# Block 1's inverse transform split twice, one of its sums moved to an accumulating transfer, and a new order of all engines

## The chip, the cores and the metric

The kernel runs on one core of one Trainium2 chip. The core has a matrix engine (TensorE, PE in the profile; its weight loads are PEld), a vector engine (VectorE, DVE), a scalar engine (ScalarE, ACT), a GpSimd engine (POOL) and SyncE (SP), which only issues transfers. Matmuls write to PSUM, and ACT or DVE carry results from there to SBUF ("evacuate"). Sixteen DMA engines move data for all queues. The metric is device time in microseconds for one execution; lower is better.

## The reference, cut to what matters

S = 2048 tokens, D = 640 channels, F = 1728. A long convolution (done with a Fourier transform) is followed by a gated FFN; each has a layer norm in front and a residual around it.

```python
def _A_ref(q, k, v, shift_k, ssm_k, ssm_D):
    k_shift = sum of k delayed by 0..3 tokens * shift_k          # four taps
    kv = k_shift * v
    y = irfft(rfft(pad(kv)) * rfft(pad(ssm_k)))[:S]               # causal long convolution
    y = y + kv * ssm_D
    return q * y
x = A_q
h = x + _A_ref(_layernorm(x), A_k, A_v, A_shift_k, A_ssm_k, A_ssm_D)
g, u = silu(_layernorm(h) @ w_gate), _layernorm(h) @ w_up
h2 = h + (g * u) @ w_down
```

## The kernel before

**Tiling.** The sequence is cut into four blocks of 512 tokens (numbers 0 to 3), and so is the convolution kernel. Each block is transformed by matmuls with a cosine and sine table into 512 complex frequencies, and the output of block i is the inverse transform of the sum over j of X(j) * C(i-j), where C are combined transforms of the convolution kernel's blocks. Within a block, token 4p + j sits on partition p in row j (j = 0 to 3). The frequencies are held in four groups of 128, one frequency per partition, each with a real and an imaginary plane, so a group of one block is 2 x 640 elements per partition, and a whole block 8 x 640 = 5120.

**Splitting.** A transform of 512 tokens can be split by the parity of the rows: the even and odd rows are transformed on their own into half of the frequencies, and sums and differences (a butterfly) give the rest. Split once, the inverse transform of a tile of 128 tokens needs 8 matmuls of 320 columns; split twice, it needs 4, and more additions. `iquads` (line 639) writes the additions of the inverse split twice; the list `R4Y` (line 360) names the blocks that use it: 2 and 3. Blocks 0 and 1 are split once: since the list `MB` (line 350) holds all blocks, `prod` (line 772) adds two DVE operations of 2560 elements by `bfly` (line 558) at the end of the block's products. They are called yb1.0 and yb1.1 for block 1. `inverse` (line 900) then has 8 or 4 matmuls per tile (lines 924 and 919).

**Sums by transfer.** `addto` (line 567) gives a sum dst += src to an accumulating transfer from SBUF to SBUF on POOL's queue instead of an addition on DVE. The list `LO` (line 343) names butterflies of which one sum is done so. For an inverse split twice that is named there, the four groups come out in another place: with the entry, tiles of rows 1 and 3 read groups that the transfer does not write, rows 0 and 2 the groups that it writes (line 905), and iquads reads those for its last difference (5) before the transfer (4) adds to them.

**Tasks and their names.** The work is recorded as a list of tasks, each numbered in the order of its creation, with the memory that it reads and writes; waits are worked out from that (`add`, line 92; `emit`, line 180). The names used here, for block i, kernel block m, row or tile j:

- `k0t`, `k0e`: transposes of the first block of K and their evacuations; `kt`/`kte`: transposes of the convolution kernel's blocks and their evacuations (1280 elements).
- `kf`/`kfe`: the forward transform of kernel block m, eight tasks of 4 matmuls, and their evacuations; `kb`: its butterflies; `kc`: combination to C.
- `tp`/`ke`/`kv`: taps by matmul, their evacuation, the product with v (DVE, line 742); `xf`/`xfe`/`xb`: forward transform of block i, its evacuations and butterflies (block 1 to 3: eight tasks of 2 matmuls; block 0: of 8).
- `pji`: the products X(j) * C(i-j) on DVE (line 777); `p02.e` and others with `e` are accumulations by transfer. `yb`: the inverse's butterfly.
- `iv`: inverse transform of a tile, then `e` evacuation (ACT), `g` gate with the normed x and residual (DVE), `m`, `s` mean and square sum (ACT, lines 840 and 842), `v`, `r` (DVE, and a power on POOL, line 837), `n` normalize (DVE), `ht` transpose to the FFN's layout (SP). For blocks 0 and 1, position 1 is row 2 and position 2 is row 1 (line 876).
- `la`/`lp`: the layer norm in front of the convolution, `lar` its power on POOL.
- `fg`, `fu`: gate and up matmuls (line 1029; 20 matmuls of 256 columns, 15 in the last group, for two halves of the block's tokens, named by the first digit after the point), `sg`, `su`, `sv`: silu and copy (ACT), `mu`: product (DVE, line 1050), `gd` a small copy; `dn`: down projection (line 1115; 28 matmuls of 320 columns), `rs`, `ra`: residual (DVE or ACT, and an accumulating transfer), `out`: store (SP).

**Order.** No engine chooses: the table `PLAN` (line 256) holds for each of the five engines the full list of task numbers in the order in which it issues them, and so also which engine does a task that two could do (for instance an evacuation). PSUM is used as four units of two banks; "units" in the table gives the unit of each PSUM tile, and a task that opens a tile waits until the last tile in that unit is evacuated. "fills" adds matmuls without use in front of a task, to keep PE running. `ub`, the buffer of the up projection, exists once: `su` waits for the `mu` before it. The order of the stages (line 348) is

```python
SEQ = "P01 K W F0 S1 P11 I1 P02 P12 P03 P13 F1 S2 P22 I2 P23 F2 S3 P33 I3 F3"
```

P stands for products, K for kernel block 3, W for the weights, F for the FFN, S for a block's loads, taps, forward transform and norm, I for its inverse. This is the order of creation; PLAN interleaves the stages, so that F0 on PE runs beside S1 and P11 on ACT and DVE.

Of the kernel before, what the change touches and what calls it, by code (L numbers as in the profile page):

```python
# [50 lines left out]
class _Graph:  # L51
# [128 lines left out]
    def emit(self, block):  # L180
# [74 lines left out]

PLAN = {
# [9 lines left out]
    "act":  # L266
# [10 lines left out]
    "dve":  # L277
# [10 lines left out]
    "pool":  # L288
        "19 17 15 16 125 165 174 158 192 183 223 225 224 342 396 362 281 371 285 401 380 289 406 389 343 293 420 415 527 466 "
        "470 561 474 552 478 579 570 684 586 591 529 705 710 698 637 732 723 641 645 750 649 741 "  # L290
        "",
    "sp":
        "0 2 3 8 4 6 10 7 230 9 11 13 14 235 296 226 12 229 297 227 481 231 167 176 228 234 295 233 194 185 482 232 364 282 373 "
        "290 391 294 286 382 480 653 652 471 563 554 467 475 479 581 572 651 734 725 638 752 646 743 642 650 798 807 801 804 "
        "810 "
        "",
    "units":
        "0131203132312001201201213230032110213023012230313133033220021021122013200230230222110332013110130232003210332301202110"
        "01310112312301210312031012210230131023033303012010313012013"
        "",  # L300
    "fills": {
        "wb0": ["zmem", 3],
        "k0t4.0": ["zmem", 1],
    },
}

# [1 line left out]
def bass_sequential_preLN__ssm_conv_h3__swiglu_ffn__prompt_kernel(  # L308
# [31 lines left out]
    DA = ((1,2),(1,3),(2,3),(3,3))  # L340
    KD = (3,)
    DD = (2,)
    LO = (('k',2),('k',3),('x',3))
    RD = (0,1,2)
    KS = (1,)
    TS = ((3,3),)
# [10 lines left out]
    HALF = (0, 1, 2, 3)  # L357
    R4K = ()
    R4X = (1,2,3)
    R4Y = (2,3)  # L360

    Q = N // 2
    kf = np.arange(Q).astype(np.float64) + 0.25
# [15 lines left out]
    with ExitStack() as es:  # L379
# [178 lines left out]
        def bfly(name, e_, o_, lo, hi, n, inplace=True, part=2):  # L558
            ops = [(hi, ALU.subtract), (lo, ALU.add)][:part]
            for k, (d, op) in enumerate(ops if inplace else ops[::-1]):  # L560
                g.add("%s.%d" % (name, k), "dve", lambda e, q, d=d, op=op: e.tensor_tensor(out=d, in0=e_, in1=o_, op=op), ("sb", n),
                      r=[e_, o_], w=[d])
# [4 lines left out]
        def addto(name, dst, src):  # L567
            return g.add(name, "pool", lambda e, n: e.dma_start(dst, src, accum_op=ALU.add, max_dma_last_dim=4096), ("acc", 2 * int(np.prod(dst.shape))),  # L568
                         r=[dst, src], w=[dst], dma=True)
# [38 lines left out]
        def quads(name, src, dst, tmp, scale, rot):  # L608
            low = (name[0], int(name[2])) in LO
            ev = 2 if low else 0  # L610
# [28 lines left out]
        def iquads(i):  # L639
            y = Y[i]  # L640

            def two(f0, c0, step):
                a = y[:, f0, c0]
                return bass.AP(a.tensor, a.offset, [list(a.ap[0]), [step * D, 2], [1, D]])

            tt2 = (("0", OS[:, 0], y[:, 0], y[:, 2], ALU.add, 2), ("1", OS[:, 1], y[:, 0], y[:, 2], ALU.subtract, 2),
                   ("2", y[:, 0], y[:, 1], y[:, 3], ALU.add, 2), ("3", y[:, 2], two(1, 1, 3), two(3, 1, -5), ALU.subtract, 2),
                   ) + ((("5", y[:, 1:4:2], OS[:], y[:, 0:3:2], ALU.subtract, 4),) if ("y", i) in LO else (
                   ("4", y[:, 1:4:2], OS[:], y[:, 0:3:2], ALU.add, 4), ("5", y[:, 0:3:2], OS[:], y[:, 0:3:2], ALU.subtract, 4)))
            for q, d, a, b, op, n in tt2:  # L650
                g.add("yb%d.%s" % (i, q), "dve", lambda e, n_, d=d, a=a, b=b, op=op: e.tensor_tensor(out=d, in0=a, in1=b, op=op), ("sb", n * D),
                      r=[a, b], w=[d])
            if ("y", i) in LO:
                addto("yb%d.4" % i, y[:, 0:3:2], OS[:])

        def kfwd(m, dst):
# [6 lines left out]
            halves("kf%d" % m, KT[m], dst, KO, D ** 0.5 / N, m)  # L663
            if ("k", m) in LO:
                bfly("kb%d" % m, dst[:, 0:2], KO[:], dst[:, 0:2], dst[:, 2:4], 4 * D, part=1)
# [87 lines left out]
        def xfwd(i):  # L753
# [7 lines left out]
            halves("xf%d" % i, kvo, x, OS, 1.0, i)  # L761
            if ("x", i) in LO:
                bfly("xb%d" % i, x[:, 0:2], OS[:], x[:, 0:2], x[:, 2:4], 4 * D, part=1)
# [8 lines left out]
        def prod(j, i):  # L772
# [3 lines left out]
            def op2(nm, d, a, b, op, n):  # L776
                g.add(nm, "dve", lambda e, n_: e.tensor_tensor(out=d, in0=a, in1=b, op=op), ("sb", n * D), r=[a, b], w=[d])  # L777
# [20 lines left out]
            for f2 in range(2):  # L798
# [13 lines left out]
                elif j:  # L812
                    op2(nm + "e", yy, yy, tacc[odd], ALU.add, 4)
                if i == j and i not in FULLY + R4Y and ("y", i) not in MB:
                    bfly("yb%d.%d" % (i, f2), y[:, f2], y[:, f2 + 2], OS[:, f2], y[:, f2 + 2], 2 * D, False)
            if i == j and i in R4Y:
                iquads(i)
            elif i == j and ("y", i) in LO:
                g.add("yb%d.0" % i, "dve", lambda e, n: e.tensor_tensor(out=OS[:], in0=y[:, 0:2], in1=y[:, 2:4], op=ALU.subtract), ("sb", 4 * D),
# [80 lines left out]
        def inverse(i):  # L900
            hold = [None]
            for j in (0, 2, 1, 3) if i in JP else range(4):
                pt = g.tile()

                full = i in FULLY
                src = Y[i][:] if full else Y[i][:, ((0, 2, 1, 3) if ("y", i) in LO else (1, 3, 0, 2))[j]] if i in R4Y else (OS[:], Y[i][:, 2:4])[(j + (("y", i) in LO)) % 2]

                def mm(e, n, pt=pt, j=j, src=src, full=full):
                    if full:
# [5 lines left out]
                        return last  # L915
                    if i in R4Y:
                        for cs in range(2):
# [10 lines left out]
                nm = "iv%d.%d" % (i, pos(i, j))  # L928
                g.add(nm, "pe", mm, ("mm", W, 16 if full else 4 if i in R4Y else 8), r=[itab[:], src] + ([nitab[:]] if full else []), pw=[pt])
                x, s = xh[i % 2][:, j, :], st1[i % 2]  # L930
# [295 lines left out]
```

## Time and profile before

| | us |
|---|---|
| three timed runs | 259.1, 260.73 (median), 261.67 |
| profiled execution, its own time | 259.3 |
| its span, first to last instruction | 257.3 |
| between them | 2.0 |

The profile is of one execution. Its rows give the start and the length in microseconds from the start of the span, the engine, the line of the kernel, and what is written and read, by the names of buffers without their number (Y, C, XH are the transforms, OS and KO scratch, ps is PSUM). In rows of the timeline a bracket gives the idle time of the engine before the row and what ended it. In the chain that ended last, a row's time is counted from the end of the row before, so that rows there are the spacing of instructions, a little less than their length: an operation of 2560 elements on DVE has a length of 1.48 and a spacing of 1.40. PE's matmuls overlap, so a busy PE need not be one that issues at its fastest.

### The profile page before, as it was taken

The numbers are of one execution on the slowest core, as the hardware profiler recorded it, in microseconds if no ns is written. First come the engines' busy times: TensorE is split into PE (matmuls) and PEld (weight loads), VectorE is DVE, ScalarE is ACT, GpSimd is POOL, SyncE is SP. The second block draws the span as 40 slices with busy tenths as digits, with TensorE's granted clock in tenths as the row PEclk, the third lists the DMA queues.
The fourth block names the chain that finished last, engine by engine and source line by source line (L and its number), as shares of the span: only waits on it lengthen the run. The fifth ranks groups of instructions, "written<-read, shape, count | busy, mean of one in ns | idle before, by whom it ended". The sixth has DMA issues, their size and how long they took to land.

```text
span 257.3 us, 5303 instructions
## 1 busy us (share of the span) xinstructions
PE 249.3 (97%) x2253; PEld 195.1 (76%) x2253; DVE 200.0 (78%) x256; ACT 184.5 (72%) x302; POOL 58.5 (23%) x56
## 2 busy tenths in 40 slices
PE   7999997999999999979999999999999999999995
PEld 4878773587888766868888866788886678888763
DVE  3689999999999998999999988999958524211242
ACT  2489999999996894577899789749981854516410
POOL 1001003082312052860030813333230314000000
PEclk9999999999999999999999999999999999999999
DMA  6998946788994058786946035497870152700011
GB/s 220 335 328 210 402 155 133 221 205 190 329 190 87 0 82 124 128 164 153 273 87 124 3 51 117 118 221 133 148 135 3 25 104 33 149 0 3 0 42 60
DMA packets 37620, 35.29 MB, mean 137 GB/s; under 512 B 21203, under 2 KB 32478, under 8 KB 37598
## 3 DMA queue, kind: packets, MB, share of 16 engines
q1 hardware_dynamic: 31792, 23.82, 33.2%
q0 software_dynamic: 5792, 11.14, 25.1%
q8 instruction: 17, 0.28, 0.5%
q14 instruction: 5, 0.04, 0.1%
q10 hardware_dynamic: 14, 0.01, 0.0%
HBM read 16.55 MB, written 2.62 MB: 75 GB/s over the span
## 4 chain that ended last, share of the span: by engine, by line
PE 62%; DVE 20%; ACT 11%; DMA 5%; issue 1%; SPq 0%; DVEq 0%
PE ps L1029 32%; PE ps L1115 16%; DVE tt L777 6%; PE ps L599 3%; DMA Y<-tt 3%; DVE Y L777 3%; PE ps L731 2%; ACT KO L455 2%; PE ps L919 2%; ACT C L455 2%; PE ps L581 2%; DVE C L777 2%; PE ps L992 2%; PE ps L619 2%; DMA k0n<-in_A_k_dram 1%; DVE gu L1050 1%
## 5 line engine op out<-in xcount | busy, mean ns | idle before, releaser
L1115 PE MATMUL ps<-Wd,gu 128*128 128x320 bf16 (+1 forms) x420 | 58.7, 300 | 0.0
L1115 PEld LDWEIGHTS ps<-Wd,gu 128*128 128x128 bf16 (+1 forms) x420 | 38.7, 97 | 18.4 <-issue 3.6
L777 DVE TENSOR_TENSOR tt<-XH,C 128x2560 bf16<-128x2560 bf16 (+1 forms) x31 | 47.8, 1571 | 1.5 <-DMA Y<-tt 0.9
L1050 DVE TENSOR_TENSOR gu<-gu,ub 128x1024 bf16<-128x1024 bf16 (+1 forms) x32 | 19.8, 620 | 26.2 <-ACT gu L1037 13.7
L1037 ACT ACTIVATE gu<-ps 128x1024 bf16<-128x1024 f32 (+1 forms) x32 | 29.4, 923 | 12.1 <-PE ps L1029 12.0
L1029 PE MATMUL ps<-hnT,GB 128*128 128x256 bf16 x280 | 34.0, 273 | 0.9 <-ACT XT L455 0.9
L1042 ACT ACTIVATE ub<-ps 128x1024 bf16<-128x1024 f32 x24 | 24.6, 1024 | 13.3 <-PE ps L1029 11.5
L1029 PE MATMUL ps<-hnT,UB 128*128 128x256 bf16 x280 | 33.8, 273 | 0.0
L1029 PEld LDWEIGHTS ps<-hnT,GB 128*128 128x128 bf16 x280 | 27.3, 98 | 4.3 <-ACT XT L455 1.0
L1029 PEld LDWEIGHTS ps<-hnT,UB 128*128 128x128 bf16 x280 | 27.3, 98 | 3.4 <-ACT KO L455 0.2
L1029 PE MATMUL ps<-hnT,GA 128*128 128x256 bf16 x240 | 28.8, 273 | 0.0
L1029 PE MATMUL ps<-hnT,UA 128*128 128x256 bf16 x240 | 28.5, 273 | 0.1
L837 POOL TENSOR_TENSOR mv<-mv,half 128x1 f32<-128x1 f32 x16 | 21.3, 1335 | 24.7 <-DVE mv L835 24.7
L1029 PEld LDWEIGHTS ps<-hnT,UA 128*128 128x128 bf16 x240 | 23.4, 98 | 3.4 <-ACT C L455 0.5
L1029 PEld LDWEIGHTS ps<-hnT,GA 128*128 128x128 bf16 x240 | 23.4, 98 | 3.2 <-DVE XH L458 0.3
L840 ACT ACTIVATE qo<-xh 128x640 bf16<-128x640 bf16 x28 | 21.0, 749 | 5.7 <-DMA xh<-in_A_q_dram 3.2
L581 PE MATMUL ps<-KT,tab 128*128 128x320 bf16 x128 | 19.6, 300 | 1.6 <-ACT K3r L455 0.7
L934 ACT ACTIVATE qo<-ps,one,st 128x640 bf16<-128x640 f32 x16 | 13.7, 886 | 9.8 <-PE ps L919 9.0
L568 POOL DMA_DIRECT2D xh<-RB x12 | 10.7, 888 | 34.7 <-DVE RB L1132 23.2
L581 PEld LDWEIGHTS ps<-KT,tab 128*128 128x128 bf16 x128 | 11.5, 98 | 8.2 <-ACT K3r L455 1.6
L837 POOL TENSOR_TENSOR st<-st,half 128x4 f32<-128x4 f32 x4 | 7.9, 1986 | 33.6 <-DVE st L832 21.8
L455 ACT ACTIVATE XH<-ps 128x640 bf16<-128x640 f32 x19 | 13.3, 736 | 1.5 <-PE ps L619 0.7
(112 smaller groups left out, 384.8 us busy)
## 6 DMA issues: line engine op xcount, KB each, us to landing
C<-US POOLq DMA_DIRECT2D x6, 640.0 KB, 5.9
kc<-in_A_ssm_k_dram SPq DMA_DIRECT2D x4, 640.0 KB, 10.6
xh<-in_A_q_dram SPq DMA_DIRECT2D x4, 640.0 KB, 5.5
out_dram<-xh SPq DMA_DIRECT2D x15, 160.0 KB, 2.0
kvo<-in_A_v_dram SPq DMA_DIRECT2D x3, 640.0 KB, 4.4
xh<-RB POOLq DMA_DIRECT2D x12, 160.0 KB, 3.0
Wd<-in_B_w_down_dram SPq DMA_DIRECT2D x1, 1280.0 KB, 7.8
C<-K3r POOLq DMA_DIRECT2D x2, 640.0 KB, 7.9
```

The lines of the kernel that those rows point to most:

```text
L455: return e.activation(out=dst[1], in_=src(), func=ACTF.Copy, scale=scale)
L568: return g.add(name, "pool", lambda e, n: e.dma_start(dst, src, accum_op=ALU.add, max_dma_last_dim=4096), ("acc", 2 * int(np.prod(dst.shap ...
L581: last = e.matmul(pt.f(c, W), tab[:, f, cs, j], src[:, j, c * W:(c + 1) * W], start=(j == js[0]), stop=(j == js[1]))
L777: g.add(nm, "dve", lambda e, n_: e.tensor_tensor(out=d, in0=a, in1=b, op=op), ("sb", n * D), r=[a, b], w=[d])
L837: g.add(name + "r", "pool", lambda e, n: e.tensor_tensor(out=dst, in0=tmp, in1=hf, op=ALU.pow), ("pp", 4), r=[tmp, half[:]], w=[dst])
L840: g.add(name + "m", "act", lambda e, n: e.activation(out=junk, in_=x, func=ACTF.Identity, scale=-1.0 / D, accum_out=sm), ("aa", D, 0), r=[ ...
L934: g.add(nm + "e", "act", lambda e, n, pt=pt, q2=q2, s=s, j=j: e.activation(out=q2, in_=pt.f2(W), func=ACTF.Identity, scale=s[:, 3, j:j + 1 ...
L1029: last = e.matmul(pt.f(q // 2, 256, o=256 * (q % 2)), w[:, c, f0:f0 + P], hnT[:, c, cols], start=(c == 0), stop=(c == NC5 - 1))
L1037: g.add("sg%d.%d%d" % (i, h, gp), "act", lambda e, n, pa=pa, gv=gv, nf=nf: e.activation(out=gv, in_=pa.f(0, 256 * nf).rearrange("p (f x) - ...
L1042: g.add("su%d.%d%d" % (i, h, gp), "act", lambda e, n, pb=pb: e.activation(out=ub[:].rearrange("p b x -> p (b x)"), in_=pb.f(0, 1024), func ...
L1050: g.add("mu%d.%d%d" % (i, h, gp), "dve", lambda e, n, gv=gv, ubv=ubv: e.tensor_tensor(out=gv, in0=gv, in1=ubv, op=ALU.mult), ("sb", 256 * ...
L1115: last = e.matmul(pt.f(c, W), gu[k, fb, col(i, j)], Wd[k, fb, c * W:(c + 1) * W], start=st, stop=sp)
```

## The change

Two entries in lists change, the filler in front of `k0t4.0` goes, and PLAN is new for all five engines and for the PSUM units. The code of the functions is the same.

```diff
-    LO = (('k',2),('k',3),('x',3))
+    LO = (('k',2),('k',3),('x',3),('y',1))
...
-    R4Y = (2,3)
+    R4Y = (1,2,3)
...
     "fills": {
         "wb0": ["zmem", 3],
-        "k0t4.0": ["zmem", 1],
     },
```

Block 1's butterfly yb1, which was two DVE operations of 2560 elements, becomes five on DVE and one transfer: yb1.0 to yb1.3 of 1280 elements, yb1.5 of 2560, and the accumulation yb1.4 (2560 elements on 128 partitions, 640 KB). Block 1's four inverse tiles have 4 matmuls each in place of 8. As four tasks more are created, all task numbers from 356 on are 4 higher. One list of PLAN shows what such a change looks like (POOL; 359 is yb1.4, 342 is la1r, and 396 before and 400 after is p02.e):

```diff
     "pool":
-        "19 17 15 16 125 165 174 158 192 183 223 225 224 342 396 362 281 371 285 401 380 289 406 389 343 293 420 415 527 466 "
+        "15 17 16 125 174 165 158 183 192 126 223 225 224 342 359 400 281 375 366 285 405 384 289 393 410 343 293 424 419 531 "
...
```

The orders that matter, written out in names. PE, from the taps of block 1 to the FFN of block 0, before:

```
tp1.2 tp1.0 iv0.0 iv0.1 tp1.4 kf2.101 iv0.2 iv0.3 kf3.001 kf2.100 kf2.111 xf1.30 xf1.31 kf2.010 kf2.001 kf2.011 kf2.110
xf1.11 kf2.000 xf1.10 xf1.01 fu0.00 xf1.20 xf1.00 fg0.00 xf1.21 fg0.01 kt3.1 kf3.100 fu0.01 kf3.101 .. kf3.010 fu0.02
```

and after:

```
tp1.0 kt2.0 iv0.1 tp1.4 tp1.2 iv0.0 kf2.001 iv0.3 kf2.111 xf1.00 kf2.011 xf1.01 xf1.31 xf1.21 iv0.2 xf1.10 kf2.010 xf1.11
kf2.101 kf2.000 kf2.100 kf2.110 xf1.30 kt3.0 kt3.1 xf1.20 fg0.00 fu0.00 fg0.01 kf3.000 fu0.01 kf3.100 .. kf3.110 fu0.02
```

ACT follows PE's order; after, kte3.0 and kf3e.001 stand behind sg0.00, and its last tasks before sg0.00 are xf1e.30, kf2e.110, iv0.2m, iv0.3m, xf1e.20, iv0.2s. PE around block 1's inverse, before and after:

```
fu0.10 fu0.12 fu0.11 iv1.1 iv1.0 fg0.13 iv1.3 dn0.0 iv1.2 dn0.0b dn0.1 dn0.2 dn0.3 fu1.00 fg1.00 tp2.2 tp2.0 tp2.4 fg1.02 xf2.30
fu0.11 dn0.0 fu0.12 iv1.1 fg0.13 dn0.0b iv1.3 iv1.0 dn0.1 iv1.2 dn0.3 dn0.2 tp2.4 fg1.00 fu1.00 fu1.01 tp2.0 tp2.2 fg1.01 xf2.30
```

DVE from the products of block 1 on, before and after:

```
p11.1c la1v mu0.02 p11.1e mu0.03 yb1.0 mu0.10 yb1.1 p02.d p02.a iv1.0g p02.c mu0.11 p02.b mu0.12 iv1.1g p12.0b ..
  .. p03.a iv1.2n p03.c mu1.00 kv2.2 kv2.0 kv2.4 p03.d iv1.3n p13.0b
p11.0e kc2.s yb1.1 p11.1b p11.1a p11.1d p11.1c yb1.0 p11.1e mu0.02 la1v yb1.2 yb1.3 mu0.03 yb1.5 mu0.10 p02.d mu0.11 p02.a p02.c p02.b ..
  .. iv1.2n p03.a mu1.00 p03.c kv2.4 p03.d iv1.3n kv2.0 kv2.2 p13.0a
```

Early on, kte0.0, k0e4 and kf0e.011 go from DVE to ACT, k0e0 and kf0e.001 from ACT to DVE, the memset of the filler's operand from POOL to DVE, and the small lp0 from DVE to POOL. On SP, ht1.1 and ht1.0 stand ahead of out0.0 (before: ht1.0, out0.0, ht1.1), and the end is out3.1, out3.2, out2.0, out2.3, out3.0, out2.2, out3.3a, out3.3c (before, the stores of block 2 stood ahead of those of block 3).

More of the change, by code (lines that the diff above doesn't have):

```diff
@@ L257 @@
     "pe":
[7 rows of a table removed]
[7 rows of a table added]
         "",
     "act":
[9 rows of a table removed]
[9 rows of a table added]
         "",
     "dve":
[9 rows of a table removed]
[9 rows of a table added]
         "",
     "pool":
-        "19 17 15 16 125 165 174 158 192 183 223 225 224 342 396 362 281 371 285 401 380 289 406 389 343 293 420 415 527 466 "
-        "470 561 474 552 478 579 570 684 586 591 529 705 710 698 637 732 723 641 645 750 649 741 "
+        "15 17 16 125 174 165 158 183 192 126 223 225 224 342 359 400 281 375 366 285 405 384 289 393 410 343 293 424 419 531 "
+        "470 474 565 478 556 482 583 688 574 590 595 709 714 702 641 727 736 754 645 745 649 653 "
         "",
     "sp":
-        "0 2 3 8 4 6 10 7 230 9 11 13 14 235 296 226 12 229 297 227 481 231 167 176 228 234 295 233 194 185 482 232 364 282 373 "
-        "290 391 294 286 382 480 653 652 471 563 554 467 475 479 581 572 651 734 725 638 752 646 743 642 650 798 807 801 804 "
-        "810 "
+        "0 2 3 8 4 235 6 10 7 9 11 13 227 296 231 12 226 295 297 14 234 228 230 485 176 167 229 233 185 486 194 232 377 368 282 "
+        "290 286 656 294 395 386 484 657 475 567 558 471 479 483 585 655 576 729 738 747 646 756 805 808 642 654 802 650 811 "
+        "814 "
         "",
     "units":
-        "0131203132312001201201213230032110213023012230313133033220021021122013200230230222110332013110130232003210332301202110"
-        "01310112312301210312031012210230131023033303012010313012013"
+        "0123102130122303101303103122223010213301211001312202202021131313332201310122130021331303333002132202031300211201000323"
+        "31110331322013012013201213012023101322020020212010232210321"
         "",
```

50 rows, old and new, of the table PLAN are left out of this document.

## The prediction

> **What bounds the kernel now.** I read the page's busy lines first, then busy time by stretches, then the chain that ended last, and last the timelines of the engines where the chain changes hands. The page:
>
> ```profile
> span 257.3 us, 5303 instructions
> PE 249.3 (97%) x2253; PEld 195.1 (76%) x2253; DVE 200.0 (78%) x256; ACT 184.5 (72%) x302; POOL 58.5 (23%) x56
> ```
>
> Busy time by stretches (time, then PE, PEld, DVE, ACT, POOL, clock, DMA share, GB/s):
>
> ```profile
> 36.00:57.00 21.00, 18.93 (x152) 12.53 (x150) 20.62 (x23) 21.00 (x40) 6.68 (x4) 1.00 0.66 163
> 57.00:82.00 25.00, 25.00 (x228) 21.14 (x226) 24.97 (x28) 23.59 (x41) 7.70 (x6) 1.00 0.88 212
> 82.00:112.00 30.00, 29.12 (x282) 22.00 (x280) 28.53 (x30) 20.53 (x35) 13.54 (x11) 1.00 0.55 86
> 112.00:160.00 48.00, 47.52 (x446) 37.93 (x444) 46.18 (x61) 41.42 (x71) 11.99 (x10) 1.00 0.56 119
> 200.00:257.30 57.30, 54.61 (x454) 42.88 (x451) 16.20 (x30) 24.44 (x40) 5.97 (x8) 1.00 0.22 47
> ```
>
> PE alone looks like the bound, with 8.0 us idle in 257.3. But from 36 to 112 DVE is idle for 1.88 us only (0.38 + 0.03 + 1.47), and ACT for none from 36 to 57. So up to some 160 us three engines are full at once and only the last 57 us belong to PE alone. The chain shows who is really last:
>
> ```profile
> 43.47 0.59 ACT C L455
> ...
> 54.81 0.71 ACT qo L840 x2
> ...
> 56.12 0.92 ACT gu L1037
> ...
> 58.52 0.73 DVE OS L634
> ...
> 77.67 0.59 DVE gu L1050
> ...
> 80.00 1.40 DVE OS L561
> ...
> 81.92 1.48 DVE Y L561
> ...
> 91.64 8.39 DMA Y<-tt
> 100.05 1.50 DVE tt L777
> ...
> 112.87 1.55 DVE kvo L742 x3
> 114.47 0.72 PE ps L619 x4
> 115.19 2.18 PE ps L1029 x20
> ...
> 149.78 1.24 PE ps L919 x8
> ...
> 198.81 1.09 PE ps L919 x8
> ```
>
> The chain runs through ACT until 57, through DVE until 114.4, and only then through PE. Block 1's butterfly (the two L561 rows) is on the DVE part. PE stands still for 2.07 us in the ACT part (18.93 of 21.00) and again where the chain leaves DVE (PE's timeline, in brackets its idle time):
>
> ```profile
> 63.62 2.36 PE L1029 MATMUL ps<-hnT,UB 128*128 128x256 bf16 x20
> ...
> 111.63 2.36 PE L1029 MATMUL ps<-hnT,GB 128*128 128x256 bf16 x20 [0.88 <-ACT XT L455]
> 114.47 0.72 PE L619 MATMUL ps<-kvo,tab 128*128 128x320 bf16 x4 [0.48 <-DVE kvo L742]
> ```
>
> **The change, part by part.** (1) PE. Block 1's inverse falls from 32 to 16 matmuls of 320 columns. Eight take 1.09 us in the chain, so one is worth 0.136 us and the sixteen 2.18 us. This is the only gain in work. The removed filler matmul is costed at 0:
>
> ```profile
> 1.14 3.47 DMA k0n<-in_A_k_dram
> 3.99 0.61 PE L502 MATMUL ps<-gu 128*128 128x512 bf16 x1
> ```
>
> The first rows of K land at 4.61 and the filler ends at 4.60: it stood inside that wait. If its absence mattered it would be by less than its own 0.61 us, in either direction.
>
> (2) DVE. Two operations of 2560 elements (1.40 in the chain, 2.80) become four of 1280 (0.73 to 0.74, 2.94) and one of 2560 (1.40): +1.54 us inside the stretch where DVE has no reserve. Otherwise both orders hold the same DVE tasks between kb0.0, where that stretch begins, and yb2.4, block 2's butterfly sum. What changes is when it begins:
>
> ```profile
> 20.02 1.49 DVE L561 TENSOR_TENSOR C<-C,KO 128x2560 bf16<-128x2560 bf16 x1 [0.18 <-ACT KO L455]
> ...
> 23.74 2.90 DVE L777 TENSOR_TENSOR tt<-XH,C 128x2560 bf16<-128x2560 bf16 x2 [0.26 <-ACT XH L455]
> ...
> 28.53 2.90 DVE L777 TENSOR_TENSOR tt<-XH,C 128x2560 bf16<-128x2560 bf16 x2 [0.29 <-ACT XH L455]
> 31.34 1.56 DVE L777 TENSOR_TENSOR Y<-tt 128x1280 bf16<-128x1280 bf16 x2
> ...
> 100.05 1.49 DVE L777 TENSOR_TENSOR tt<-XH,C 128x2560 bf16<-128x2560 bf16 x1 [0.90 <-DMA Y<-tt]
> ...
> 114.33 1.48 DVE L777 TENSOR_TENSOR C<-tt 128x2560 bf16<-128x2560 bf16 x1
> 115.73 0.44 DVE L981 TENSOR_SCALAR qo<-xh,mv 128x640 bf16<-128x640 bf16 x1
> ...
> 148.22 1.49 DVE L651 TENSOR_TENSOR Y<-OS,Y 128x2560 bf16<-128x2560 bf16 x1
> ```
>
> At 20.02 kb0.0 waits for four of the eight evacuations kf0e. The last of the four is now the seventh and not the eighth: -0.59, one evacuation. At 23.74 and 28.53 DVE waits for ACT's evacuations of xf0, ahead of which fewer evacuations of transposed K are now put: -0.55 for the two waits. The copy that DVE gives to ACT (kte0.0) and the memset that it takes from POOL lie ahead of this stretch and count 0. I take -1.2 in all, with 0 and -1.9 as ends (nothing; one evacuation more). Of later waits I take as many as before, 1.88. Net at yb2.4: +1.54 - 1.2 = +0.3 us.
>
> (3) The place of block 2's k·v products. Before, the three kv2 end at 114.42 (112.87 + 1.55). After, p03.d (1.40) and iv1.3n (0.36, from 115.73 to the next start at 116.09) stand ahead of the last two: 114.42 + 0.3 + 1.76 = 116.5. The forward transform xf2 needs all three. PE does one FFN group more ahead of it (fg1.01 and fu1.01 in place of fg1.02), which costs 2.18 (20 matmuls, the row at 115.19) and uses up just what (1) saved. Without its stalls near tp2.4 and fg1.02 (0.88 and 0.48 idle; some 1.7 from start to start) PE would be there at 114.47 - 1.7 = 112.8; so it waits in the new order too. With that group already done PE leaves this point, on the old scale of work, at 116.5 - 2.18 = 114.3: 0.15 ahead and not 2.18.
>
> (4) ACT between 33 and 66. The old order mixes the eight xf1 with FFN groups; the new one runs iv0, kf2 and xf1 in one piece and FFN behind it, where each xf1 gives PE 0.27 us (2 x 0.136) and ACT 0.59. Ahead of sg0.00 ACT loses kte3.0 (1.13), su0.00 (0.92), iv0.3s (0.81) and kf3e.001 (0.59), and gains kte0.0 (1.13) and iv0.2s (0.81):
>
> ```profile
> 32.60 1.13 ACT KT L455
> ...
> 39.00 0.81 ACT qo L842 x2
> ...
> 52.71 0.92 ACT ub L1042
> ```
>
> That is -1.5, so sg0.00 starts between 54.6 and, if the 1.5 goes in new waits, 56.1; I take 55.0. Evacuation kf2e.110, which frees the PSUM unit for fg0.00, ends 2.8 us earlier (two L840 at 0.71, one evacuation, one L842), at 52.2. From there to fu0.02 PE has four FFN groups (8.72) and eight kf3 (4.37): 65.2. Before it was there at 63.62 with the same tasks done, so it is 1.6 late. In the sum that costs nothing while DVE is the later one at xf2: 112.8 + 1.6 = 114.4 against 116.5. Were DVE early it would cost the 1.6.
>
> (5) The accumulating transfer yb1.4, 640 KB on POOL's queue, stands behind la1r (a power of 4 elements) and ahead of p02.e:
>
> ```profile
> 77.76 1.40 POOL L837 TENSOR_TENSOR st<-st,half 128x4 f32<-128x4 f32 x1 [1.72 <-DVE st L835]
> ...
> 142.60 4.42 POOL L837 TENSOR_TENSOR st<-st,half 128x4 f32<-128x4 f32 x1 [9.58 <-DVE st L835]
> ```
>
> It waits for yb1.5, which reads what it writes. Before, yb1.1 ended at 83.40. Ahead of yb1.5's end DVE has 1.54 more of butterfly, no mu0.10 (0.59) and the earlier start: 83.4 + 1.54 - 0.59 - 1.2 = 83.1. With the 8.39 us of the nearest transfer (same target) it lands at 91.5. PE wants it at iv1.0, ahead of which it has, counted from iv1.1's old start at 82.73, iv1.1 and iv1.3 in half (1.09), fg0.13 (15 x 0.109 = 1.64) and dn0.0 (28 x 0.136 = 3.81): 89.3, and 90.9 with the 1.6 of (4). So PE waits 0.6, or 2.2 if it isn't late, and either way is there at 115.0 for xf2, where (3) swallows it. Behind it p02.e goes out at about its old 91.64, 10 us later. I take 0, ends 0 and +1.1 (the third rival).
>
> Queue SP: the transposes ht1.1 and ht1.0 now stand ahead of the store out0.0, which helps. At the end four stores of block 2 are put behind out3.2, shortly before the last store, on the same queue. I take +0.2, ends 0 and +0.6 (0.15 each).
>
> **Sum.** At iv2.1 (149.78 before) DVE's sum allows 149.8 + 0.3 = 150.1, PE by itself 149.78 - 0.15 = 149.6. So +0.3 there. From there PE's work is the same, its order too but for swaps inside F2 and F3, and the chain stays on PE from there on with hardly a wait, so the shift goes to the end: +0.3 + 0.2 = +0.5. The profiled execution took 259.3 us; that is 1.4 below the median 260.73 of the three runs (259.1, 260.73, 261.67). With it the middle of the four is 260.0, and on that I put the sum: **260.5 us**. A measurement of this kernel can tell about 1%, 2.6 us, from no change.
>
> **Rivals.** *Gain kept.* If DVE loses the 1.88 us that it idled between 36 and 112 and starts 0.7 earlier still, kv2 ends at 113.9 and PE (114.4) is the bound at xf2: on the old scale 112.2 and not 114.47, -2.2. 260.0 - 2.2 + 0.2 = 258.0. For it: PE has no other work added. Against it: half of DVE's idle time is the 0.90 for the transfer Y<-tt, and between p02.e and its waiter DVE has only one more short task (iv1.0g) than before. Chance 0.25.
>
> *DVE waits for ACT* (slower). In (4) ACT delivers just when DVE asks. From the end of the first products (32.9, less 1.2: 31.7) to xb1.0 DVE has seven operations of 1.40, two of 2.74 and short ones, 19.5 in all, so it is there at 51.2; xf1e.30 stands just ahead of kf2e.110 and ends at 52.2 - 0.6 = 51.6. From there each us that ACT is later goes through kv2 and yb2.4 to the end. If the 1.5 of (4) is lost in waits and the kf3 evacuations are late by PE's 1.6 as well: +3.1, or 260.0 + 3.1 + 0.5 = 263.6. For it: ACT is busy for 21.00 of 21.00 us between 36 and 57. Against it: its sum is smaller than before. Chance 0.27.
>
> *The accumulate is late.* One power of this kind took far longer than the rest:
>
> ```profile
> L837 POOL TENSOR_TENSOR mv<-mv,half x16: 540/862/5208, 41.0 to 217.7; 128x1 f32<-128x1 f32 x16
> ```
>
> Then la1r, which starts at about 80, ends at 85.2, the transfer lands at 93.6, 2.7 after PE wants it (90.9). The wait at xf2 swallows 2.1 of that (114.4 against 116.5), 0.6 stays, and I allow 0.5 for the evacuation and the products that queue behind iv1.0 on ACT and DVE: +1.1, or 261.6. Up to 2.1 us late it costs nothing. For it: DVE runs additions without a break behind la1v, as at 142.60. Against it: so it did at 77.76. Chance 0.10. [...]
>
> **Chances.** Forecast 0.38, its own range 259.3 to 262 (the ends of start, accumulate and stores). Over all: 257.6 to 264.0. Faster by over 1% (under 258.1): 0.18, most of the first rival. Slower by over 1% (over 263.3): 0.23, most of the second. Within: 0.59.
>
> **What would show it.** Block 1's inverse in sixteen matmuls; idle time of PE of some 2 us before xf2, ended by DVE kvo; kv2 ending near 116.5; yb2.4's addition ending within 1 us of 150; fu0.02 later than 63.6. Wrong would be: PE without idle time from 100 to 120; DVE idle for over 3 us between 36 and 112; PE waiting over 2 us for the transfer Y<-OS; or idle time of PE after 163, where I count none.

## The result, and the profile after

The changed kernel takes 267.34 us (median of 6 runs, 266.18 to 267.91) against 260.91 us for the kernel before beside it: a ratio of 1.0246, 95% interval 1.0204 to 1.0287. The forecast was 260.5, so it is slower by 6.4 us where almost no change was expected. The profiled execution took 266.18 us, its span is 264.2. Two profiles below (the transfer ahead of la1r, 264.69 us, and the old start, 263.76) are of slow executions, 4 to 5 us above their medians, and are read only up to 142 us. The page:

```profile
span 264.2 us, 5274 instructions
PE 249.6 (94%) x2236; PEld 193.4 (73%) x2236; DVE 201.5 (76%) x260; ACT 184.5 (70%) x302; POOL 66.6 (25%) x56
```

PE has 17 matmuls fewer, and POOL is busy for 8.1 us more with the same 56 instructions. Busy time by stretches (columns as before):

```profile
36.00:57.00 21.00, 18.22 (x144) 12.00 (x143) 20.41 (x23) 20.97 (x39) 6.47 (x4) 1.00 0.70 160
57.00:82.00 25.00, 25.00 (x222) 21.46 (x220) 24.75 (x27) 22.98 (x39) 7.94 (x7) 1.00 0.87 191
82.00:112.00 30.00, 24.85 (x186) 16.98 (x184) 25.03 (x29) 18.31 (x33) 15.87 (x11) 0.89 0.57 93
112.00:160.00 48.00, 47.72 (x491) 38.84 (x488) 44.28 (x52) 37.50 (x59) 15.81 (x10) 1.00 0.56 113
```

Only the row from 82 to 112 is new in kind: PE and DVE both stand still for 5 of 30 us, and the granted clock is 0.89. The chain that ended last names the place:

```profile
79.86 9.31 POOL st L836
89.17 5.85 DMA Y<-OS
...
95.16 1.22 PE ps L918 x4
...
120.37 1.20 DVE kvo L741 x2
...
148.26 5.72 POOL st L836
153.98 2.91 DMA xh<-RB
```

POOL was not on this chain before. Line 836 is the power (837 before). Rows of the engines' timelines at this place:

```profile
79.59 0.17 DVE L834 TENSOR_SCALAR st<-st 128x4 f32<-128x4 f32 x1
...
79.86 9.35 POOL L836 TENSOR_TENSOR st<-st,half 128x4 f32<-128x4 f32 x1 [3.80 <-DVE st L834]
...
81.47 1.50 DVE L650 TENSOR_TENSOR Y<-OS,Y 128x2560 bf16<-128x2560 bf16 x1
...
85.47 2.83 DVE L776 TENSOR_TENSOR Y<-XH,C 128x5120 bf16<-128x5120 bf16 x1
...
88.34 1.49 DVE L776 TENSOR_TENSOR Y<-Y 128x2560 bf16<-128x2560 bf16 x1
...
89.17 1.24 POOL L567 DMA_DIRECT2D Y<-OS  x1
...
95.16 1.22 PE L918 MATMUL ps<-Y,itab 128*128 128x320 bf16 x4 [5.15 <-DMA Y<-OS]
96.31 5.66 PE L1114 MATMUL ps<-Wd,gu 64*128 64x320 bf16 x28
...
97.33 0.49 DVE L940 TENSOR_TENSOR xh<-xh,qo 128x640 bf16<-128x640 bf16 x1 [3.57 <-ACT qo L933]
```

la1r, a power of four elements per partition, takes 9.35 us; before it took 1.40. The transfer yb1.4 behind it could have gone out when yb1.5 ended (81.47 + 1.50 = 82.97) and goes out at 89.17, PE waits for it for 5.15 us, and DVE then waits 3.57 us for the evacuation of the same tile. From there everything is late: the kv2 products end at 121.57 (120.37 + 1.20) and not at 114.42 as before. With la2r, the same power for block 2, the chain goes through POOL a second time.

### The profile page after: what moved, and what is told of

Same layout as the page of the kernel before. It is cut to its first block, busy times and chain, and to the rows that moved or that the text cites. A ratio compares the mean times of both kernels' runs of the same rounds, so it can differ in the third digit from the quotient of the medians.

```text
span 264.2 us, 5274 instructions
## 1 busy us (share of the span) xinstructions
PE 249.6 (94%) x2236; PEld 193.4 (73%) x2236; DVE 201.5 (76%) x260; ACT 184.5 (70%) x302; POOL 66.6 (25%) x56
## 4 chain that ended last, share of the span: by engine, by line
PE 45%; DVE 35%; POOL 9%; DMA 6%; ACT 2%; issue 2%; SPq 0%; DVEq 0%; ACTq 0%
PE ps L1028 24%; PE ps L1114 15%; DVE tt L776 12%; POOL st L836 6%; DVE Y L776 4%; DVE XH L633 3%; DVE C L560 3%; POOL mv L836 2%; DMA v<-in_A_v_dram 2%; DMA Y<-OS 2%; PE ps L580 2%; PE ps L991 2%; PE ps L918 2%; DVE kvo L741 2%; DVE gu L1049 2%
## 5 line engine op out<-in xcount | busy, mean ns | idle before, releaser
L1114 PE MATMUL ps<-Wd,gu 128*128 128x320 bf16 (+1 forms) x420 | 60.4, 305 | 0.0
L1114 PEld LDWEIGHTS ps<-Wd,gu 128*128 128x128 bf16 (+1 forms) x420 | 39.4, 99 | 20.1 <-issue 4.4
L836 POOL TENSOR_TENSOR mv<-mv,half 128x1 f32<-128x1 f32 x16 | 20.3, 1269 | 37.1 <-DVE mv L834 37.1
L836 POOL TENSOR_TENSOR st<-st,half 128x4 f32<-128x4 f32 x4 | 17.2, 4312 | 35.1 <-DVE st L831 21.3
L567 POOL DMA_DIRECT2D xh<-RB x12 | 11.3, 938 | 38.3 <-ACT RB L1130 21.3
L567 POOL DMA_DIRECT2D C<-US x6 | 7.2, 1290 | 31.0 <-DVE US L776 31.0
```

Of the source, the lines that this page charges most:

```text
L836: g.add(name + "r", "pool", lambda e, n: e.tensor_tensor(out=dst, in0=tmp, in1=hf, op=ALU.pow), ("pp", 4), r=[tmp, half[:]], w=[dst])
L1114: last = e.matmul(pt.f(c, W), gu[k, fb, col(i, j)], Wd[k, fb, c * W:(c + 1) * W], start=st, stop=sp)
```

## The experiments

**Theory 1**, a guess that the runs below try: la1r, a POOL instruction that reads SBUF, gets nowhere while DVE runs additions or products with two inputs in SBUF one right behind the other (79.66 to 88.30 in the changed kernel, where la1r ends at 89.21); it waits for the first pause, and the transfer waits behind la1r. **Rival A:** the power is slow by itself. **Rival B:** the transfer is too late in any case, since it is issued late or takes long. For the rest of the difference: the new order by itself (above all its first part, **order theory**), or the split by itself. The twelve kernels ran in four groups on four chips, where the kernel before takes 258.3 to 258.5 us (260.9 beside the result); each ratio is to the kernel before on the same chip.

**A pause for la1r.** One swap on DVE puts yb1.5 right behind yb1.3, whose result it needs.

```diff
-la1v yb1.2 yb1.3 mu0.03 yb1.5 mu0.10
+la1v yb1.2 yb1.3 yb1.5 mu0.03 mu0.10
```

> The changed kernel with two tasks swapped on DVE: yb1.5 ahead of mu0.03. yb1.5 reads what yb1.3 has just written, so DVE has to stop for a moment between them at about 81.2. Theory 1 (a POOL instruction that reads SBUF is shut out while DVE runs two-input operations without a break; the power la1r and so the accumulate behind it and block 1's evacuations wait for the first break): la1r ends about 0.9 us after that break, at 82.1 and not 89.2, the accumulate is issued when yb1.5 ends (82.7) and lands at 88.5 to 91, PE waits for it less than 1.5 us, the granted clock is 1.00 throughout, and the time falls by 5 to 7 us to 260.5 to 262. Rival A (the power is slow for another reason, POOL's own work or the transfers): la1r stays over 5 us long and the time stays at 267. Rival B (the transfer is too late in any case): la1r is short but PE still waits over 3 us at iv1.0, time 264 to 266.

Ratio 1.0078 (1.0051 to 1.0106), 1.7% below the changed kernel: some 4.4 us, where 5 to 7 were expected. The timeline, POOL and DVE:

```profile
80.10 1.55 DVE L650 TENSOR_TENSOR Y<-Y 128x1280 bf16<-128x1280 bf16 x2
80.28 2.27 POOL L836 TENSOR_TENSOR st<-st,half 128x4 f32<-128x4 f32 x1 [3.22 <-DVE st L834]
81.69 1.49 DVE L650 TENSOR_TENSOR Y<-OS,Y 128x2560 bf16<-128x2560 bf16 x1
```

Between yb1.3's end (81.65) and yb1.5's start (81.69) DVE pauses for 0.04 us. la1r ends 0.90 us behind that pause, after 2.27 us and not 9.35, and PE does not wait for the transfer. Rivals A and B fall.

**The transfer ahead of la1r** on POOL.

```diff
-la1r yb1.4 p02.e
+yb1.4 la1r p02.e
```

> The changed kernel with the accumulate yb1.4 ahead of the power la1r on POOL; DVE's order is untouched. Theory 1: the accumulate is issued at 83.0 and lands at 89 to 91; la1r starts at about 84.2, still ends 0.9 us after DVE's break at 88.3, so block 1's evacuations begin at 89.3 as in the changed kernel, but iv1.0 no longer waits for the transfer: 261 to 262.5. Rival A (POOL's power is slow by itself, 9 us): it ends at 93.5, evacuations and PE wait for that, time 267 or more. Rival B (the transfer itself is too late): 264 to 266.

Ratio 1.0041 (1.0013 to 1.0069).

```profile
84.36 1.20 POOL L567 DMA_DIRECT2D Y<-OS  x1 [6.77 <-DVE Y L650]
85.11 5.19 POOL L836 TENSOR_TENSOR st<-st,half 128x4 f32<-128x4 f32 x1
...
90.87 1.26 PE L918 MATMUL ps<-Y,itab 128*128 128x320 bf16 x8
```

la1r is still slow (5.19), but nothing that matters is behind it: iv1.3 and iv1.0 run without a wait at 90.87.

**A POOL instruction that only writes** in la1r's place.

```diff
-lambda e, n: e.tensor_tensor(out=dst, in0=tmp, in1=hf, op=ALU.pow)
+lambda e, n: e.memset(dst, 0.04) if name == "la1" else e.tensor_tensor(out=dst, in0=tmp, in1=hf, op=ALU.pow)
```

> The changed kernel with block 1's power la1r replaced by a POOL memset of a constant to the same 4 elements: it reads nothing from SBUF and waits for the same addition. Left out: the scale of block 1's first layer norm (a constant stands in for it). Theory 1: POOL writes are not shut out, the memset takes 0.1 to 0.3 us at 79.9 though DVE runs on without a break, the accumulate is issued at 83.0 and lands at 89 to 91, time 260 to 261.5. Rival A (POOL is slow to start or finish anything there): the instruction or its signal is late as before, over 265. Rival B (transfer too late in any case): 264 to 266.

Ratio 1.0041 (1.0018 to 1.0063). The timeline also shows the taps of block 2:

```profile
80.97 0.10 POOL L836 MEMSET st<- 128x4 f32 x1 [3.13 <-DVE st L834]
84.40 1.20 POOL L567 DMA_DIRECT2D Y<-OS  x1 [3.33 <-DVE Y L650]
...
90.92 1.26 PE L918 MATMUL ps<-Y,itab 128*128 128x320 bf16 x8
...
115.25 1.28 DVE L741 TENSOR_TENSOR kvo<-XT,kvo 128x1024 bf16<-128x1024 bf16 x2
...
116.59 1.26 PE L618 MATMUL ps<-kvo,tab 128*128 128x320 bf16 x8 [0.99 <-DVE kvo L741]
```

This kernel leaves out the true scale of block 1's first norm. The write takes 0.10 us beside the same additions, so this POOL instruction, which only writes, is not held up there. Against the changed kernel (1.0246) the three kernels win 1.7 to 2.1% by their ratios, which is 4.4 to 5.3 of the 6.4 us.

**Matmuls without use in PE's wait**, to keep its clock.

```diff
+"iv1.0": ["tab0", 20],
```

> The changed kernel with 20 matmuls of 512 columns without use in front of iv1.0, in the time in which PE waits for the accumulate (20 x 0.216 = 4.3 us). Theory 1 adds: of the loss, PE's wait is 5.3 us and another 2.3 us are matmuls at half the clock after it (granted clock 0.5 from 93.1 to 99.9). With PE kept at work the clock stays 1.00, iv1.0 and dn0.1 take 4.4 and not 6.6 us: time 265.0. Rival: what follows is set by DVE anyway and the clock costs nothing: 267.

Ratio 1.0222 (1.0152 to 1.0291, four runs).

```profile
90.12 4.49 PE L502 MATMUL ps<-tab 128*128 128x512 bf16 x20 [0.20 <-ACT qo L934]
94.93 0.72 PE L919 MATMUL ps<-Y,itab 128*128 128x320 bf16 x4 [0.32 <-DMA Y<-OS]
95.58 3.95 PE L1115 MATMUL ps<-Wd,gu 64*128 64x320 bf16 x28
...
117.84 1.29 DVE L742 TENSOR_TENSOR kvo<-XT,kvo 128x1024 bf16<-128x1024 bf16 x2
```

In the changed kernel the granted clock is at half (0.50) from 93.10 for 6.83 us, at the end of PE's wait and behind it, and the 28 matmuls behind iv1.0 take 5.66 us. Here the clock stays whole in the profiled execution and they take 3.95. The kv2 products end 39.65 us behind the start of la1v (79.48 to 119.13), and in the changed kernel 41.98 (79.59 to 121.57). So up to this point the half clock costs 2.3 us, as was expected, on top of the wait. The four runs cannot tell how much of it reaches the end: their interval holds the changed kernel's 1.0246 as well as a gain of 2.3 us (0.9%).

**One swap of neighbours, both ways.** In the kernel before, mu0.02 stands behind la1v; in the changed one it stands ahead. The first run puts it ahead in the kernel before, the second puts it behind in the changed one.

```diff
-p11.1c la1v mu0.02 p11.1e mu0.03
+p11.1c mu0.02 la1v p11.1e mu0.03
```

> The kernel before with mu0.02 put ahead of la1v on DVE, so that la1v has only long additions and products behind it, as in the changed kernel. By Theory 1 la1r now takes over 5 us and ends 0.90 us after the first pause between two additions (p02.a to p02.c, near 87.5): 9 to 10 us. If the 1.40 us of before came from something else than what stands behind la1v, it stays near 1.4. The time stays the same, since the transfer p02.e behind it waits for p02.c anyway.

One execution: 260.15 us, la1r 10.08 us.

```profile
77.81 0.16 DVE L835 TENSOR_SCALAR st<-st 128x4 f32<-128x4 f32 x1
...
78.06 10.08 POOL L837 TENSOR_TENSOR st<-st,half 128x4 f32<-128x4 f32 x1 [1.62 <-DVE st L835]
...
84.42 2.82 DVE L777 TENSOR_TENSOR Y<-XH,C 128x5120 bf16<-128x5120 bf16 x1
...
89.15 0.49 DVE L941 TENSOR_TENSOR xh<-xh,qo 128x640 bf16<-128x640 bf16 x1 [1.91 <-ACT qo L934]
```

la1r ends at 88.14, again 0.90 us behind the end of DVE's last operation without a pause (84.42 + 2.82 = 87.24). So in the kernel before, too, by this one execution, a single place in DVE's order decides between 1.4 and 10 us. The mirror:

```diff
-p11.1e mu0.02 la1v yb1.2
+p11.1e la1v mu0.02 yb1.2
```

> The changed kernel with one swap of two neighbours on DVE: mu0.02 stands behind la1v and not ahead of it, as in the kernel before; it is the mirror of the run that put mu0.02 ahead of la1v in the kernel before. By Theory 1 la1r gets through at the end of mu0.02 and takes about 1.4 us, the transfer goes out when yb1.5 ends (about 84), PE does not wait for Y<-OS, and the ratio is 1.002 to 1.006. If the place of la1v among its neighbours does not decide, la1r takes over 5 us again and the ratio is 1.02 or more.

Ratio 1.0055 (1.0032 to 1.0078).

```profile
81.39 0.17 DVE L834 TENSOR_SCALAR st<-st 128x4 f32<-128x4 f32 x1
81.47 0.69 DVE L1049 TENSOR_TENSOR gu<-gu,ub 128x1024 bf16<-128x1024 bf16 x1
81.65 1.40 POOL L836 TENSOR_TENSOR st<-st,half 128x4 f32<-128x4 f32 x1 [2.91 <-DVE st L834]
82.07 1.55 DVE L650 TENSOR_TENSOR Y<-Y 128x1280 bf16<-128x1280 bf16 x2
...
85.66 1.24 POOL L567 DMA_DIRECT2D Y<-OS  x1 [2.60 <-DVE Y L650]
```

la1r takes 1.40 us and ends 0.89 us behind mu0.02 (82.16). The swap alone takes back most of the loss. Why POOL gets in behind mu0.02 stays open: no pause shows there (the next addition starts at 82.07), and behind three other products of this line it did not get in (81.13, 82.87 and 84.87 in the changed kernel). So Theory 1's first pause does not cover this case.

**The order alone.** The new order, block 1 split once: yb1.0 behind la1v, yb1.1 behind mu0.03.

```diff
-LO = (('k',2),('k',3),('x',3),('y',1))
+LO = (('k',2),('k',3),('x',3))
-R4Y = (1,2,3)
+R4Y = (2,3)
-la1v yb1.2 yb1.3 mu0.03 yb1.5 mu0.10
+la1v yb1.0 mu0.03 yb1.1 mu0.10
```

> The new order with block 1's inverse transform split once (32 matmuls, two butterfly additions of 2560, no transfer for it): the order alone. If Theory 1 holds, la1r is shut out again, as behind la1v stand additions without a break: over 5 us, ended within 1 us of the first break between two-input additions; but no transfer of the inverse is behind it, so PE does not wait for Y<-OS. If the loss of the changed kernel is that wait, this kernel is near the ones with the wait removed: ratio 1.005 to 1.015 (they had 1.004, and here are 2.2 us more of matmuls and 1.5 us less of additions). If the order is bad by itself, whatever the transform, the ratio is 1.02 or more. If only the split is bad, it is 1.00 or less.

Ratio 1.0114 (1.0086 to 1.0142).

```profile
80.53 1.49 DVE L560 TENSOR_TENSOR OS<-Y 128x2560 bf16<-128x2560 bf16 x1
80.71 2.20 POOL L836 TENSOR_TENSOR st<-st,half 128x4 f32<-128x4 f32 x1 [2.91 <-DVE st L834]
82.40 0.43 DVE L1049 TENSOR_TENSOR gu<-gu,ub 128x512 bf16<-128x512 bf16 x1 [0.38 <-ACT ub L1045]
```

The expected long la1r did not come, for the reason that Theory 1 gives: DVE paused for ACT at 82.02, and la1r ended 0.89 us later. The time is in the range expected for the order without the transfer's wait: the order loses some 1.1% by itself, and the split on top of it gains 0.4 to 0.7% (1.0078 to 1.0041 in the three kernels without la1r's delay).

**The split alone.** The old order with yb1.0 to yb1.5 and yb1.4 put in by hand, and block 1's tiles as 1, 3, 0, 2.

```diff
-mu0.03 yb1.0 mu0.10 yb1.1 p02.d
+mu0.03 yb1.0 yb1.1 mu0.10 yb1.2 yb1.3 yb1.5 p02.d
-iv1.1 iv1.0 fg0.13 iv1.3 dn0.0 iv1.2 dn0.0b dn0.1
+fg0.13 iv1.1 iv1.3 dn0.0 dn0.0b iv1.0 dn0.1 iv1.2
-la1r p02.e
+la1r yb1.4 p02.e
```

> The old order with block 1 split twice and the sum by transfer: the algebra alone, with the tiles of block 1's inverse put in the order 1, 3, 0, 2 and the transfer behind la1r. The old place of la1v makes la1r quick (1.4 us), so the transfer goes out at the end of yb1.5, about 85, and lands at 91.5, about when PE wants it. DVE has 1.54 us more, PE 2.18 less. If DVE sets the pace up to the taps of block 2, as the prediction has it, the ratio is 1.003 to 1.010. If PE sets it, the 2.18 us come out as a gain: 0.992. If la1r is slow here too (9 us), PE waits for Y<-OS and the ratio is over 1.015.

Ratio 1.0297 (1.0267 to 1.0328), outside every expectation.

```profile
77.80 1.40 POOL L837 TENSOR_TENSOR st<-st,half 128x4 f32<-128x4 f32 x1 [1.71 <-DVE st L835]
85.40 1.23 POOL L568 DMA_DIRECT2D Y<-OS  x1 [6.20 <-DVE Y L651]
...
110.95 4.13 PE L1029 MATMUL ps<-hnT,UA 128*128 128x256 bf16 x20 [6.15 <-DMA hnT<-qo]
```

la1r is quick and the transfer is in time, as expected. But fu1.00 waits 6.15 us for the transpose ht1.0: tile 0 now ends behind the transfer, and the hand order had too little other work ahead of fu1.00. So this run does not tell what the split is worth in the old order.

**The old start with the new rest**, with the transfer ahead of la1r.

```diff
-all engines up to fu0.02 and kb3.0: the new order
+all engines up to fu0.02 and kb3.0: the order of the kernel before
-la1r yb1.4 p02.e
+yb1.4 la1r p02.e
```

> The old order of all engines up to about 72 (through fu0.02 and kb3.0), then the new order with block 1 split twice and the transfer ahead of la1r. In the old part PE had stalls of 4.1 us between 36 and 57, in the new one 6.2. If that stretch is what is left of the loss (order theory), this kernel is 2 us faster than the ones with the transfer's wait removed: ratio 0.994 to 0.998, faster than before. If DVE sets the pace up to the taps of block 2, whatever PE does (the prediction's step 3), the ratio is 1.000 to 1.004. The clock stays whole up to 72 by either.

Ratio 1.0036 (1.0018 to 1.0053). Busy time:

```profile
36.00:57.00 21.00, 18.92 (x156) 12.84 (x156) 20.63 (x24) 21.00 (x41) 7.43 (x4) 1.00 0.68 170
57.00:82.00 25.00, 23.79 (x208) 19.70 (x207) 24.96 (x28) 21.14 (x38) 5.56 (x5) 1.00 0.84 206
```

PE does more from 36 to 57 (18.92 us against 18.22 after, so it stands still there for 2.1 and 2.8 us, not for the 4.1 and 6.2 of the expectation), and stands still later. The time is that of the transfer ahead of la1r with the new start (1.0041), so the order theory falls as to the first part. DVE is full in both stretches, which fits that it sets the pace up to the taps of block 2; that was not tried by itself. The reverse, the new start with the old rest:

```diff
-all engines up to fu0.02 and kb3.0: the order of the kernel before
+all engines up to fu0.02 and kb3.0: the new order
```

> The reverse: the new order up to the same tasks, then the old order with block 1 split once. If the new first part costs what PE loses in it, the ratio is 1.005 to 1.010, with a half clock of 3.41 us near 43. If it costs nothing because DVE sets the pace behind it, the ratio is 0.999 to 1.003.

Ratio 1.0093 (1.0072 to 1.0115). The ratio lies where it was expected if the first part costs what PE loses in it. But it cannot be taken for that, since the seam makes a wait that neither kernel has: la1v on DVE waits for la1.3s on ACT (DVE's waits from 36 to 118: the sum, how often, the longest). It stays inconclusive.

```profile
DVE st L834 <- ACT qo L841: 2.8, 1, 2.8
```

**Matmuls without use from 38 to 44**, with the transfer ahead of la1r.

```diff
+"kf2.111": ["tab0", 2], "xf1.00": ["tab0", 3], "kf2.011": ["tab0", 4], "xf1.31": ["tab0", 1],
```

> The changed kernel with the transfer ahead of la1r (1.004 before) and ten matmuls without use put into the stretch from 38 to 44, where PE waits for ACT and where the clock then fell to half for 3.41 us. If the fall comes from PE's idle time there and costs time, the clock is whole from 36 to 57 and the time falls by 0.6 to 1.0 us, ratio 1.000 to 1.002. If it comes from it but ACT sets the pace there anyway, the clock is whole and the ratio stays at 1.004. If PE's idle time is not the cause, the half clock stays.

Ratio 1.0013 (0.9990 to 1.0036), against 1.0041 without them.

```profile
36.00:57.00 21.00, 19.75 (x182) 13.20 (x177) 20.63 (x24) 21.00 (x39) 4.64 (x4) 1.00 0.70 177
```

In seven of the nine profiles of the new start without these fillers the clock fell to half for 3.41 us near 43 (the order alone: 0.92 from 36 to 57). With the fillers it is whole, and so it is by the mean clock of the runs: 0.999 or 1.000 in eleven of twelve, against one of eleven without them. The ratio is in the range expected for a fall that costs time (1.000 to 1.002); by these two ratios the half clock costs some 0.3%, but their intervals overlap, so it may also cost nothing.

**The kv2 products first**, with the transfer ahead of la1r.

```diff
-kv2.4 p03.d iv1.3n kv2.0 kv2.2
+kv2.4 kv2.0 kv2.2 p03.d iv1.3n
```

> The changed kernel with the transfer ahead of la1r, and the products kv2.0 and kv2.2 put ahead of p03.d and iv1.3n on DVE: step 3 of the prediction undone by itself. If DVE at the taps of block 2 sets the end, the wait of PE of 0.6 to 1.2 us ahead of xf2 goes and the ratio falls from 1.004 to 1.000 to 1.002. If PE catches up or loses it again behind, the ratio stays at 1.004.

Ratio 1.0111 (1.0073 to 1.0148): worse than with the transfer ahead of la1r alone, and outside both expectations.

```profile
114.68 0.69 DVE L741 TENSOR_TENSOR kvo<-XT,kvo 128x1024 bf16<-128x1024 bf16 x1 [0.84 <-ACT XT L454]
115.59 0.69 DVE L741 TENSOR_TENSOR kvo<-XT,kvo 128x1024 bf16<-128x1024 bf16 x1 [0.22 <-ACT XT L454]
```

DVE now waits 1.06 us for ACT's evacuations of the taps; p03.d had filled that time. kv2 ends at 116.28, hardly earlier than with the new order (116.53 in the write-only run), and p03.d's work comes on top.

## Why the prediction was wrong

(1) Held: the sixteen matmuls and the filler are gone, 2253 to 2236.

(2) Shown in part. The two waits at 23.74 and 28.53 are gone in the changed kernel. kb0.0 starts at 19.09 after 20.02, 0.9 earlier where 1.2 was taken, but its start differs from execution to execution: 18.96 to 20.92 in ten profiles of the new start, 19.28 to 20.06 in four of the old. So the earlier start is not shown. With la1r out of the way (the write-only run) block 2's butterfly sum yb2.4 ends at 150.06, where within 1 us of 150 was predicted; with a start so uncertain, so close a match is in part luck.

(3) Held in its place, not in its size. In the same run kv2 ends at 116.53 (115.25 + 1.28), predicted 116.5, and PE waits there, ended by DVE kvo, though for 0.99 us and not 2 (0.63 with the pause for la1r, 0.45 with the transfer ahead of it). In the changed kernel itself this wait is gone, since PE is late as well. There was nothing to win back here: with kv2 put first the kernel gets slower.

(4) Held in part. sg0.00 starts at 53.87 (predicted 55.0; before 55.85) and fu0.02 at 64.13 (predicted 65.2; before 63.62). Both come about 1.1 us earlier than predicted, and fu0.02 is 0.5 later than before and not 1.6. Not foreseen: the half clock of 3.41 us in this stretch (0.92 from 36 to 57 in the write-only run). The profiled execution of the changed kernel does not have it. But four of its six runs have a mean granted clock of 0.980 or 0.981 and not 0.986, as 3.41 us more of half clock would give by an estimate (half of 3.41 in a span of 265 is 0.006), and they took 267.1 to 267.9 us against 266.2 and 266.3.

(5) This step failed, and the prediction's own sign of being wrong came: PE waits for the transfer Y<-OS for over 2 us (5.15). "I take 0, ends 0 and +1.1" rested on la1r at 1.4 us. yb1.5 ended when predicted (82.97 against 83.1) and the transfer took less than taken (5.85 against 8.39), but la1r held POOL's queue until 89.17: landed at 95.02, not 91.5. The right mechanism was the rival with chance 0.10, and it too was sized too small, for four reasons. It took 5.2 us from another power of this line; la1r took 9.35, and 1.4 to 10.1 in the runs above. It let the wait at xf2 swallow 2.1 us, but that wait is 1.0 us and less, as (3) shows. DVE, which sets the end there, waits for the same tile through the gate iv1.0g (3.57 us), and no later wait of PE swallows that. And it had no term for the half clock that came with PE's wait (0.50 for 6.83 us). From the start of la1v to the end of kv2 it takes 35.78 us in the write-only run (80.75 to 116.53), 39.65 with la1r's delay but the clock kept whole, and 41.98 in the changed kernel: 3.9 us for the delay and 2.3 for the clock. The forecast's +0.2 for the stores at the end (0.15 each) was the author's estimate, and no run shows it: from DVE's last operation on the chain to the end it takes 2.65 us before (254.65 to 257.3) and 2.63 in the changed kernel (261.57 to 264.2).

The argument against the rival was "so it did at 77.76", one quick la1r. The run with mu0.02 ahead of la1v shows what that was worth: the quick one hung on its neighbour, and the change moved just that neighbour. At la1r's new place the power, which reads SBUF, took 9.35 us, and the instruction that only writes took 0.10. The row at 77.76 stays unexplained, but with another neighbour it said nothing about that place.

The span of the changed kernel is 6.6 us longer than that of the write-only run (257.6). 5.2 of them are there at the end of yb2.4 (155.29 against 150.06); the other 1.4 come behind it, where la2r takes 5.75 us and the transfer of the residual waits behind it. In the run with matmuls in PE's wait la2r takes 1.54 us, and from the end of yb2.4 (152.83) to the end it takes 107.6 us, as in the write-only run (107.5), and not 108.9 as in the changed kernel. That la2r is the whole cause was not tried.

With la1r's delay taken away and nothing else, the change costs 0.4 to 0.8% in four kernels (the pause, the transfer ahead, the write, the mirror), and 0.1% with the fillers near 43, against +0.2% in the forecast's sum. Which part of the order costs the rest was not found. "Gain kept" did not come true: no kernel that was tried was measured faster than the kernel before. Within the new order the split does gain 0.4 to 0.7% (1.0 to 1.9 us, where PE's work is 2.18 less), but the order alone loses 1.1%.

## What to carry to other kernels

Before a transfer is put into a queue behind a small GpSimd instruction that reads SBUF (la1r took 9.35 us here in place of 1.40), read what DVE runs at that moment: if it is additions of two SBUF inputs without a pause, take the time to DVE's next pause as an estimate of the small instruction's length (la1r ended 0.89 to 0.91 us behind the start of such a pause), and put the transfer ahead of it (1.0041 here against 1.0246) or a dependent pair on DVE behind its source (1.0078). One quick instance in a trace is not a price; look at all instances of the line and ask what stood beside each. A wait is swallowed by a later wait only if no engine that ends the later one has waited for the same thing. And a long wait of PE is not the whole price: here 5.15 us of it came with 6.83 us at half clock, which cost 2.3 us more (41.98 against 39.65).

## What the runs showed of the hardware

la1r ends 0.89 to 0.91 us behind the end of the DVE operation ahead of the first pause: 88.30 to 89.21 in the changed kernel, 81.65 to 82.55, 82.02 to 82.91 and 87.24 to 88.14 in the runs above. A pause of 0.04 us was enough (88.30 to 88.34 and 81.65 to 81.69). Where mu0.02 stands directly behind la1v, it ends 0.89 or 0.90 us behind mu0.02 although no pause shows (kernel before: 78.26 to 79.16).

The clock fell to half without any long wait of PE: near 43 PE had only waits of up to 1.0 us each, for ACT (write-only run, granted clock 0.88 from 34 to 48). In the changed kernel's profiled execution the same stretch (18.22 of 21.00 us busy) ran at 1.00, in the order alone (18.26 us busy) at 0.92, so nearly the same busy time came with two clocks. The two lengths at half clock are 3.41 and 6.83 us, the second twice the first; why the same stretch falls in one execution and not in another was not shown.
